# Rewriting the head of an SSM kernel generator: small constants moved to GpSimd, imaginary parts first, the sine table loaded behind the exponential

## The chip, the cores and the metric

The kernel runs on one core of a Trainium2 chip. The time is device time in microseconds of one execution; "before" was run three times. Five engines work side by side, each through its own queue in program order: TensorE (PE, matmuls), VectorE (DVE), ScalarE (ACT), GpSimd (POOL) and SyncE (SP, which here issues nearly all DMAs). They wait for each other by semaphores.

## The reference, cut to what matters

Four layers on x of shape [1, 2048, 512]: A, B, A, B, each added to its input after a layer norm. A is a sliding, dilated local attention (32 heads of 16, window 8, dilation 2). B is a state-space convolution: for each of 512 channels a kernel K of 2048 taps is generated from 128 complex states, and then convolved with the input by an FFT. The change touches only the start of the generation of K, which serves both B layers:

```python
dt = jnp.exp(log_dt)[:, None]
A = A_re + 1j * A_im
logdA = dt * A
dB = dt * (B_re + 1j * B_im)
P = jnp.exp(logdA[:, :, None] * l[None, None, :])     # l = 0 .. 2047
K = jnp.einsum("dn,dnl,dn->dl", Cc, P, dB).real       # Cc = C_re + 1j * C_im
```

## The kernel before

`k_gen` builds K. Its head forms z = exp(dt·A) for all channels and states as one real and one imaginary plane of 128 x 512 (128 states on the partitions, 512 channels in the row). In the order of the code (line numbers of before):

- `build_a_consts` (L83 to L126) makes the constants of layer A ahead of `k_gen`: POOL writes integer ramps with iota, and DVE compares them: `ident` (L88), `nident` (L90), the indicator matrices, `maskrow`, `slot_sel` and `slot_mask` (L95 to L124).
- SP loads `raw_A_re`, `raw_A_im`, `raw_B_re`, `raw_B_im`, `raw_C_re`, `raw_C_im` (L1010), then the first block of x, then fills `w_dram` in DRAM with 4 MB of zeros (L1396, from a zeroed piece of `xnT`, memset at L1380), then the second block of x and the two halves of the query and key weights into `kT_ext` (L245, L246).
- ACT takes the exponential of `log_dt` (`dt_row`, L1025). A matmul with `ident` turns it into a column per channel block (L1027), and DVE multiplies `ident` by it into `dt_diag` (L1029).
- `turned_by` (L1018 to L1022) transposes a raw tile with four matmuls against `dt_diag` or `ident`, so that the A and C parts come out scaled by dt. A_re goes first, then A_im, then B and C.
- ACT forms `a_re` = exp(dt·A_re) (L1040, in the tile `sq_z`) and `turn` = dt·A_im / 2π (L1041, in the tile `ws`). DVE rounds the turn off with a magic number: `t1` from PSUM (L1042), the remainder in `ws` (L1043), its absolute value in `t2` (L1044). ACT takes the two sines (L1045, L1046); the compiler puts the load of the sine table just ahead of the first. DVE multiplies sines and exponential into `sq_z` (L1055, L1056): that is z.
- `build_b_consts` (L610 ff.) makes the index columns for the sine tables of the FFT: POOL iotas, DVE integer steps into `pk` (L621 to L629), DVE steps into `aux` (L633 to L637) and, in its inner function `rest`, into `w_off`, `w_eo` and the two `off_` tiles (L647 to L654), and ACT steps (L641) that use them.

What follows is an order written out by hand, `ORDERK`: one letter per step, and each step issues its instructions on its engine. z is squared eleven times (ACT squares L1059, DVE L1063 and L1066). ACT copies some powers into `pow_t` (L1073, L1078) and others into `B_t` (L1075); SP copies one row of each `pow_t` level beside itself (`power_copy`, L1081). DVE builds two tables of products, `B_t` and `A_t` (all L1084), where each level k of `A_t` reads `pow_t[k]` with its copied row. Between them stand the layer norm of x (statistics and application on ACT, `ln_nb` on DVE L1154), its transposes on PE (L1170), the query and key projections (L1180), and PE's products of the two tables (L1242), which give K. The manual schedule covers DVE, ACT, PE and SP; the placement of POOL's instructions is left to the scheduler.

Of the kernel before, what the change touches and what calls it, by code (L numbers as in the profile page):

```python
# [10 lines left out]
ACT = mybir.ActivationFunctionType  # L11
ALU = mybir.AluOpType
AX = mybir.AxisListType
PSUM = bass.MemoryType.PSUM
F32 = mybir.dt.float32
BF16 = mybir.dt.bfloat16
I32 = mybir.dt.int32
I16 = mybir.dt.int16
ET = mybir.EngineType

P = 128
S = 2048
D = 512
H = 32
DH = 16
W = 8
# [3 lines left out]
EXP_LN = "natural_log_exp_and_others"  # L30
MAN = {ET.DVE, ET.Activation, ET.PE, ET.SP}
SIN_SHRINK = 1.0 - 4e-7
# [50 lines left out]
def build_a_consts(tc, nc, cpool, tpool):  # L83
    c = {}
    it = tpool.tile([P, P], I32, name="iota_id")
    nc.gpsimd.iota(it[:], pattern=[[1, P]], base=0, channel_multiplier=-1)
    ident = cpool.tile([P, P], BF16, name="ident")
    nc.vector.tensor_scalar(ident[:], it[:], 0, None, ALU.is_equal)  # L88
    nident = cpool.tile([P, P], BF16, name="nident")
    nc.vector.tensor_scalar(nident[:], it[:], 0, -1.0, ALU.is_equal, ALU.mult)  # L90
    c["ident"], c["nident"] = ident, nident
    u = tpool.tile([P, 8], I32, name="iota_ind")
    nc.gpsimd.iota(u[:], pattern=[[-16, 8]], base=0, channel_multiplier=1)
    m1 = tpool.tile([P, 8], F32, name="ind_m1")
    nc.vector.tensor_scalar(m1[:], u[:], 0, None, ALU.is_ge)  # L95
    m2 = tpool.tile([P, 8], F32, name="ind_m2")
    nc.vector.tensor_scalar(m2[:], u[:], 15, None, ALU.is_le)
    ind8 = cpool.tile([P, 8], BF16, name="ind8")
    nc.vector.tensor_tensor(ind8[:], m1[:], m2[:], ALU.mult)
    c["ind8"] = ind8  # L100
    rows = cpool.tile([1, P], BF16, name="rows")
    nc.vector.memset(rows[:], 0.0)
    nc.vector.memset(rows[:, 0:1], 1.0)
    c["e0"] = rows[:]
    mv = tpool.tile([1, NA, W], I32, name="iota_mask")
    nc.gpsimd.iota(mv[:], pattern=[[1, NA], [-2, W]], base=0, channel_multiplier=0)
    mrow = cpool.tile([1, NA, W], BF16, name="maskrow")
    nc.vector.tensor_scalar(mrow[:], mv[:], 0, -1e9, ALU.is_lt, ALU.mult)
    c["maskrow"] = mrow
    c["zrow"] = rows[:, 64:128]  # L110
    ind = cpool.tile([P, NDT * H], BF16, name="ind32")
    nc.gpsimd.memset(ind[:], 0.0)
    diag = bass.AP(tensor=ind.tensor, offset=ind[:].offset, ap=[list(ind[:].ap[0]), [H + 8, NDT], [1, 8]])
    nc.vector.tensor_tensor(diag, m1[:].unsqueeze(1).to_broadcast([P, NDT, 8]), m2[:].unsqueeze(1).to_broadcast([P, NDT, 8]), ALU.mult)
    c["ind"] = ind[:].rearrange("p (t h) -> p t h", t=NDT)
    sv = tpool.tile([4, 4, H], I32, name="iota_slot")
    nc.gpsimd.iota(sv[:], pattern=[[-1, 4], [0, H]], base=0, channel_multiplier=1)
    slot = cpool.tile([4, 4, H], BF16, name="slot_sel")
    nc.vector.tensor_scalar(slot[:], sv[:], 0, None, ALU.is_equal)
    c["slot"] = slot[:].rearrange("k a h -> k (a h)")  # L120
    mc = tpool.tile([4, max(NCOL), W], I32, name="iota_slot_mask")
    nc.gpsimd.iota(mc[:], pattern=[[4, max(NCOL)], [-2, W]], base=0, channel_multiplier=1)
    keep = cpool.tile([4, max(NCOL), W], BF16, name="slot_mask")
    nc.vector.tensor_scalar(keep[:], mc[:], 0, -1e9, ALU.is_lt, ALU.mult)  # L124
    c["mask"] = keep
    return c  # L126
# [66 lines left out]
class LayerA:  # L193
# [33 lines left out]
    def front_open(self):  # L227
        tc = self.tc
        self.fctx = ExitStack()
        l = self.layer  # L230
        self.fp = self.fctx.enter_context(tc.tile_pool(name=f"a{l}_front", bufs=2, side="right"))
        self.nc.gpsimd.memset(self.kT[:, :, 0:14, 0:1], 0.0)
# [369 lines left out]
def iota_f32(nc, pool, name, n, step=1, base=0, channel_multiplier=0, parts=P):  # L602
    ti = pool.tile([parts, n], I32, name=name + "_i")
    nc.gpsimd.iota(ti[:], pattern=[[step, n]], base=base, channel_multiplier=channel_multiplier)
    tf = pool.tile([parts, n], F32, name=name)
    nc.scalar.copy(tf[:], ti[:])
    return tf


def build_b_consts(nc, cpool, tmp, w2_dram):  # L610
    C = {}
    EQ = P // 4
    base = tmp.tile([P, EQ, 16], I32, name="w2_base", tag="w2_base")
# [4 lines left out]
    d4i = iota_f32(nc, tmp, "d4i", 2)  # L618
    nc.gpsimd.iota(base[:], pattern=[[16, EQ], [4096, 16]], base=8, channel_multiplier=0)
    t_i = tmp.tile([P, 8], I32, name="pk_t")  # L620
    nc.vector.tensor_scalar(t_i[:, 0:1], pi_i[:], 63, 2, ALU.bitwise_and, ALU.logical_shift_right)  # L621
    nc.vector.tensor_scalar(t_i[:, 1:2], pi_i[:], 6, None, ALU.logical_shift_right)
    nc.vector.tensor_scalar(t_i[:, 2:3], pi_i[:], 3, None, ALU.bitwise_and)
    nc.vector.tensor_scalar(t_i[:, 3:4], pi_i[:], 31, 1, ALU.bitwise_and, ALU.logical_shift_right)
    nc.vector.tensor_scalar(t_i[:, 4:5], pi_i[:], 1, None, ALU.bitwise_and)
    nc.vector.tensor_scalar(t_i[:, 5:6], pi_i[:], 5, 1, ALU.logical_shift_right, ALU.bitwise_and)
    nc.vector.tensor_scalar(t_i[:, 6:7], pi_i[:], 63, 1, ALU.bitwise_and, ALU.logical_shift_left)
    nc.vector.tensor_copy(t_i[:, 7:8], pi_i[:])
    pk = tmp.tile([P, 8], F32, name="pk"); nc.vector.tensor_copy(pk[:], t_i[:])  # L629
# [3 lines left out]
    nc.vector.tensor_tensor(aux[:, 0:1], pk[:, 6:7], rik, ALU.add)  # L633
    nc.vector.tensor_scalar(aux[:, 1:2], pf, 2.0, 1.0, ALU.mult, ALU.add)
    C["p21"] = aux[:, 1:2]
    dmask_m = aux[:, 4:6]
    nc.vector.tensor_scalar(dmask_m, d4i[:], d4m, 2.0 / 4096.0, ALU.is_equal, ALU.mult)  # L637
# [6 lines left out]
    def rest():  # L644
        def off_cols(name, rcol, v00, v10, v01, v11):
            o = tmp.tile([P, 2], F32, name=name)
            nc.vector.tensor_scalar(o[:, 0:1], rcol, float(v10 - v00), float(v00), ALU.mult, ALU.add)  # L647
            nc.vector.tensor_scalar(o[:, 1:2], rcol, float(v11 - v01), float(v01), ALU.mult, ALU.add)
            return o
# [3 lines left out]
        nc.vector.scalar_tensor_tensor(eo[:], ak, 512.0, d4k, ALU.mult, ALU.mult)  # L653
        nc.vector.tensor_tensor(off[:], off[:], eo[:].to_broadcast([P, 2]), ALU.add)  # L654
# [42 lines left out]
    return C, head, rest  # L697
# [282 lines left out]
def k_gen(tc, nc, ident, ins, kd, la, x_v, lnst, zero, b_consts):  # L980
# [3 lines left out]
    with ExitStack() as ctx:  # L984
# [8 lines left out]
        late = {}  # L993
        la.front_open()
# [3 lines left out]
        def nat(ap):  # L998
            return ap.rearrange("p (q g) -> p q g", g=4)
# [8 lines left out]
        for name in ("A_re", "A_im", "B_re", "B_im", "C_re", "C_im"):  # L1008
            raw[name] = sp.tile([P, 4, N], BF16, name="raw_" + name)
            nc.sync.dma_start(raw[name][:], ins[name].rearrange("(t p) n -> p t n", p=P))  # L1010
# [4 lines left out]
        nc.gpsimd.memset(Bt[:, 0, :, 0, :], 1.0)  # L1015
        nc.gpsimd.memset(Bt[:, 1, :, 0, :], 0.0)

        def turned_by(name, rhs):  # L1018
            pt = pst.tile([P, 4, P], F32, name="pt")
            for t in range(4):  # L1020
                nc.tensor.matmul(pt[:, t, :], lhsT=raw[name][:, t, :], rhs=rhs(t), start=True, stop=True)
            return pt[:].rearrange("p g q -> p q g")  # L1022

        dtr = sp.tile([4, P], BF16, name="dt_row")
        nc.scalar.activation(dtr[:], ldt[:], ACT.Exp)  # L1025
        pdt = pst.tile([P, 4, P], F32, name="pt")
# [4 lines left out]
        C, head, rest = b_consts(sp)  # L1031
# [5 lines left out]
        a_re, turn = cur[0][:, 0], ws[:, 2]  # L1037
        p_re = turned_by("A_re", by_dt)
        p_im = turned_by("A_im", by_dt)
        nc.scalar.activation(nat(a_re), p_re, ACT.Exp)  # L1040
        nc.scalar.mul(nat(turn), p_im, 1.0 / TWO_PI)  # L1041
        nc.vector.tensor_scalar(nat(t1[:]), p_im, 1.0 / TWO_PI, MAGIC, ALU.mult, ALU.add)  # L1042
        nc.vector.scalar_tensor_tensor(turn, t1[:], MAGIC, turn, ALU.subtract, ALU.subtract)  # L1043
        nc.vector.scalar_tensor_tensor(t2[:], turn, -1.0, turn, ALU.mult, ALU.max)  # L1044
        nc.scalar.activation(sn, turn, ACT.Sin, scale=TURN)  # L1045
# [3 lines left out]
        steps, w2_store = rest()  # L1049
# [303 lines left out]
def kernel(  # L1353
# [27 lines left out]
    with tc.tile_pool(name="ctmp", bufs=1) as tmp:  # L1381
        consts = build_a_consts(tc, nc, cpool, tmp)
# [3 lines left out]
    nc.gpsimd.memset(lnst["mh"][:], -0.5)  # L1386
# [6 lines left out]

    with tc.manual_schedule(engines=MAN):
        C = k_gen(tc, nc, consts["ident"], ins, kd, la, x_v, lnst,
                  lambda: nc.sync.dma_start(w2_dram.rearrange("p e c -> p (e c)").rearrange("p (n x) -> p n x", x=1024),  # L1396
                                            zt.unsqueeze(1).to_broadcast([P, P * P // 1024, 1024])),
                  lambda sp: build_b_consts(nc, cpool, sp, w2_dram))
# [61 lines left out]
    with tc.manual_schedule(engines=MAN):  # L1460
        la.front_open()
        ln, agg, pts = {}, {}, {}
# [88 lines left out]
```

## Time and profile before

| what | value |
|---|---|
| median of 3 runs (lowest, highest) | 412.89 us (412.36, 413.35) |
| the profiled execution: time, span | 412.14 us, 410.3 us |
| busy: DVE, ACT, PE | 384.2 us (94%), 326.7 us (80%), 322.0 us (78%) |
| busy: POOL | 46.0 us (11%), 52 instructions |
| granted TensorE clock, mean | 0.938 |
| DMA | 54.17 MB, mean 132 GB/s |

A line of the timeline reads: start in us, duration in us, engine and line, operation, output tile <- input tiles, shape and type of each, number of instructions, and in brackets the idle time of that engine just before, with what ended it. A line of the windows holds, for a stretch A:B, its length, then the busy time and number of instructions of PE, PE weight loads, DVE, ACT and POOL, then the granted TensorE clock, the mean busy share of the 16 DMA engines and GB/s. A line of the DMA issues ends with the median time from issue to landing.

### The profile page before, as it was taken

What the parts mean: (1) busy time and instruction counts of PE and PEld (TensorE: products, weight loads), DVE (VectorE), ACT (ScalarE), POOL (GpSimd) and SP (SyncE); (2) the same over time, 40 slices, a digit from 0 to 9 for tenths busy, and PEclk for the clock granted to TensorE, in tenths of its full rate; (3) what the DMA queues carried; (4) which work ended last, traced back from release to release, by engine and by line L of the source; (5) the groups of instructions that cost most, each with busy time, mean ns of one, the idle gap of its engine ahead of it and who ended that gap; (6) DMA issues with size and microseconds to landing.
All of it is one profiled execution on the core that took longest, in us unless ns stands there. A gap on an engine that the chain in (4) does not pass through costs nothing.

```text
span 410.3 us, 14708 instructions
## 1 busy us (share of the span) xinstructions
PE 322.0 (78%) x6467; PEld 227.0 (55%) x6513; DVE 384.2 (94%) x498; ACT 326.7 (80%) x562; POOL 46.0 (11%) x52
## 2 busy tenths in 40 slices
PE   2000168899899888789988889999998999897794
PEld 2000026567535555566887778543466677566784
DVE  7999999999999999998899989888988999989993
ACT  5999999897556589898999978874656658889972
POOL 3000400000299300001400000000000020000000
PEclk9555569999999999999999999999999999999998
DMA  7930742113015856583245595830043028504516
GB/s 229 388 113 13 84 82 72 33 41 91 13 39 123 213 169 180 159 339 105 71 164 182 180 307 141 311 127 2 0 116 92 3 71 343 158 3 150 161 30 181
DMA packets 62322, 54.17 MB, mean 132 GB/s; under 512 B 33869, under 2 KB 50738, under 8 KB 60978
## 3 DMA queue, kind: packets, MB, share of 16 engines
q1 hardware_dynamic: 62250, 53.22, 42.8%
q8 instruction: 51, 0.84, 0.9%
q14 instruction: 13, 0.11, 0.1%
q10 hardware_dynamic: 8, 0.00, 0.0%
HBM read 30.15 MB, written 13.24 MB: 106 GB/s over the span
## 4 chain that ended last, share of the span: by engine, by line
PE 35%; ACT 18%; DVE 17%; issue 7%; DMA 3%; SPq 2%; DVEq 0%; ACTq 0%
PE pk L1242 5%; DVE pav L458 5%; PE pq L389 5%; DVE prod L333 4%; ACT a1s L774 4%; PE pp L1180 4%; ACT ub L851 3%; PE pp L273 3%; PE pq L216 3%; PE pq L494 2%; DVE t L835 2%; PE pb L869 2%; PE po L483 2%; PE L L341 2%; DMA v_ext<-v_ext 1%
## 5 line engine op out<-in xcount | busy, mean ns | idle before, releaser
L458 DVE TENSOR_TENSOR pav<-attn,v_ext 128x4096 bf16<-128x4096 bf16 (+1 forms) x34 | 73.1, 2168 | 1.2 <-DMA v_ext<-v_ext 0.8
L333 DVE TENSOR_TENSOR prod<-qT,kT_ext 128x4096 bf16<-128x4096 bf16 x29 | 67.1, 2337 | 1.6 <-ACT qT L218 1.1
L1170 PE MATMUL pt<-ident,x_blk 128*128 128x128 bf16 x64 | 6.3, 241 | 42.6 <-DMA w_dram<-w_q 41.1
L1084 DVE TENSOR_TENSOR A_t<-A_t,pow_t 128x1024 bf16<-128x1024 bf16 (+4 forms) x46 | 38.2, 870 | 0.2
L483 PEld LDWEIGHTS <-pav 64*128 64x128 bf16 x1664 | 26.2, 95 | 15.1 <-DVE pav L458 8.5
L483 PE MATMUL po<-ident,pav 64*128 64x64 bf16 x1664 | 29.0, 190 | 6.6 <-DVE pav L458 3.9
L494 PE MATMUL pq<-wop,oT 128*128 128x512 bf16 x122 | 31.6, 379 | 2.5 <-issue 1.9
L851 ACT CAST ub<-pb 128x1024 bf16<-128x1024 f32 x32 | 32.3, 1091 | 0.1
L391 ACT CAST v_ext<-pq 128x512 bf16<-128x512 f32 x32 | 18.8, 586 | 17.0 <-PE pq L389 16.0
L792 PE MATMUL pb<-a1s,w_sb 128*128 128x64 bf16 x768 | 28.0, 193 | 5.4 <-ACT a1s L774 2.3
L389 PE MATMUL pq<-wv,xnT 128*128 128x512 bf16 x121 | 30.1, 379 | 0.6 <-ACT kgs L1250 0.3
L1180 PE MATMUL pp<-xnT,kT_ext 128*128 128x512 bf16 x87 | 25.0, 405 | 7.0 <-ACT qT L1185 2.9
L1170 PEld LDWEIGHTS <-x_blk 128*128 128x128 bf16 x64 | 4.8, 108 | 45.0 <-ACT x_blk L188 43.6
L792 PEld LDWEIGHTS <-w_sb 128*128 128x128 bf16 x768 | 25.0, 98 | 8.0 <-issue 5.2
L774 DVE CAST a1s<-pb 128x1024 bf16<-128x1024 f32 x21 | 25.0, 1217 | 4.1 <-PE pb L785 4.1
L774 ACT CAST a1s<-pb 128x1024 bf16<-128x1024 f32 x27 | 26.4, 1052 | 2.3 <-PE pb L785 2.2
L1242 PEld LDWEIGHTS <-A_t 128*64 128x64 bf16 (+1 forms) x512 | 21.8, 103 | 4.1 <-issue 0.6
L1242 PE MATMUL pk<-B_t,A_t 128*64 128x84 bf16 (+1 forms) x512 | 23.6, 201 | 0.1
L216 PE MATMUL pq<-xnT,kT_ext 128*128 128x512 bf16 x89 | 22.8, 379 | 0.5 <-issue 0.3
L494 PEld LDWEIGHTS <-oT 128*128 128x128 bf16 x128 | 12.4, 98 | 14.0 <-ACT oT L485 1.1
L485 ACT CAST oT<-po 128x512 bf16<-128x512 f32 x26 | 15.0, 577 | 6.0 <-PE po L483 5.9
L389 PEld LDWEIGHTS <-xnT 128*128 128x128 bf16 x128 | 11.6, 97 | 14.1 <-issue 1.9
(258 smaller groups left out, 871.9 us busy)
## 6 DMA issues: line engine op xcount, KB each, us to landing
w_sb<-w_dram SPq DMA_DIRECT2D x8, 1024.0 KB, 6.7
w_dram<-xnT SPq DMA_DIRECT2D x1, 4096.0 KB
kf_ring<-kf_dram SPq DMA_DIRECT2D x13, 256.0 KB, 4.4
kf_ring<-kf_dram SPq DMA_DIRECT2D x26, 128.0 KB, 3.7
v_ext<-v_ext SPq DMA_DIRECT2D x4, 784.0 KB, 6.3
x_blk<-in_A_x_dram SPq DMA_DIRECT2D x4, 512.0 KB, 3.9
kT_ext<-in_A_wqkv_dram SPq DMA_DIRECT2D x4, 512.0 KB, 9.9
x_sb<-in_A_x_dram SPq DMA_DIRECT2D x4, 512.0 KB, 5.2
```

The lines of the kernel that those rows point to most:

```text
L216: nc.tensor.matmul(pq[:], lhsT=self.wqk[:, dt, ft * P:(ft + 1) * P], rhs=self.xnT[:, dt, q * 512:(q + 1) * 512], start=(dt == 0), stop=(dt ...
L333: nc.vector.tensor_tensor(pr, self.qT[q][:, ft].unsqueeze(1).to_broadcast([P, W, 4, P]), kap, ALU.mult)
L389: nc.tensor.matmul(pp[:], lhsT=xnT[:, dt, a * P:(a + 1) * P], rhs=wv[:, dt, :], start=(dt == 0), stop=(dt == NDT - 1))
L458: nc.vector.tensor_tensor(pv[:, i], attn[:, n % 4].unsqueeze(2).to_broadcast([P, W, DH // parts, H]), vap, ALU.mult)
L483: nc.tensor.matmul(po[:, h, 0, i * nt + ft, :], lhsT=pvf[rows, i, w, ft * P:(ft + 1) * P], rhs=ident[rows, rows], start=(w == 0 and ft + i ...
L494: nc.tensor.matmul(pw[:], lhsT=oT[:, ftp, :], rhs=self.wo[:, ftp, :], start=False, stop=(ftp == NDT - 1))
L774: (self.nc.scalar.copy if eng == "act" else self.nc.vector.tensor_copy)(dst, src)
L792: nc.tensor.matmul(p2[:, j, :], lhsT=self.w2[:, ec * EC + j, :], rhs=a1s[:, ec * EC + j, :], start=True, stop=True)
L851: nc.scalar.copy(ub[:], p2)
L1084: return lambda: nc.vector.tensor_tensor(*args)
L1180: nc.tensor.matmul(pps[kind, b, ft][:], lhsT=la.wqk[:, dt, c:c + P], rhs=la.xnT[:, dt, b * 512:(b + 1) * 512], start=(dt == 0), stop=(dt = ...
L1242: nc.tensor.matmul(o, lhsT=lhs, rhs=Bt[:, ri, c * CH + ql].rearrange("p b g -> p (b g)"), start=(not half and j % 4 == 0 and ri == 0), sto ...
```

## The change

- `build_a_consts` moves into `k_gen` and is split in three. At once come the iota for `ident` and, now on POOL, `ident` itself; `iotas()` issues the other ramps behind the exponential of `log_dt`; `rest()` (called `a_rest`) makes the remaining constants, now on POOL, behind those of `build_b_consts`.
- `build_b_consts` is split likewise: its iotas first, then `keys` (DVE, into `pk`), `keyed` (`aux`, now on POOL) and `rest` (offsets, now on POOL; one fused DVE step becomes two POOL steps).
- POOL joins the engines of the manual schedule for `k_gen`, so that its instructions stand in the order of the code. The memsets of `kT_ext` (`front_zero`), `ln_mh` and `B_t` come behind the iotas.
- A_im is loaded and transposed ahead of A_re; `turn` stands ahead of the exponential on ACT.
- `t1` reads `turn` from SBUF instead of A_im from PSUM.
- The load of the sine table is written out, behind the exponential.

On the engines' queues: 20 instructions fewer on DVE, 21 more on POOL, as many as before on PE, ACT and SP. The scheduler puts the memset of the tile `Wp` between the first iota and `ident`, and that of `WpJ` among the offsets. `ORDERK` is unchanged.

```diff
-def build_a_consts(tc, nc, cpool, tpool):
-    c = {}
+def build_a_consts(nc, cpool, tpool, c):
     it = tpool.tile([P, P], I32, name="iota_id")
     nc.gpsimd.iota(it[:], pattern=[[1, P]], base=0, channel_multiplier=-1)
     ident = cpool.tile([P, P], BF16, name="ident")
-    nc.vector.tensor_scalar(ident[:], it[:], 0, None, ALU.is_equal)
+    nc.gpsimd.tensor_scalar(ident[:], it[:], 0, None, ALU.is_equal)
...
+    def iotas():
+        nc.gpsimd.iota(u[:], pattern=[[-16, 8]], base=0, channel_multiplier=1)
...
+    def rest():
+        nc.gpsimd.tensor_scalar(nident[:], it[:], 0, -1.0, ALU.is_equal, ALU.mult)
+        m1 = tpool.tile([P, 8], F32, name="ind_m1")
+        nc.gpsimd.tensor_scalar(m1[:], u[:], 0, None, ALU.is_ge)
...
+    return iotas, rest
...
 def build_b_consts(nc, cpool, tmp, w2_dram):
...
+    def keys():
+        nc.vector.tensor_scalar(t_i[:, 0:1], pi_i[:], 63, 2, ALU.bitwise_and, ALU.logical_shift_right)
...
+    def keyed():
+        nc.gpsimd.tensor_tensor(aux[:, 0:1], pk[:, 6:7], rik, ALU.add)
...
-            nc.vector.tensor_scalar(o[:, 0:1], rcol, float(v10 - v00), float(v00), ALU.mult, ALU.add)
+            nc.gpsimd.tensor_scalar(o[:, 0:1], rcol, float(v10 - v00), float(v00), ALU.mult, ALU.add)
...
-        nc.vector.scalar_tensor_tensor(eo[:], ak, 512.0, d4k, ALU.mult, ALU.mult)
-        nc.vector.tensor_tensor(off[:], off[:], eo[:].to_broadcast([P, 2]), ALU.add)
+        nc.gpsimd.tensor_scalar(eo[:], ak, 512.0, None, ALU.mult)
+        nc.gpsimd.tensor_tensor(eo[:], eo[:], d4k, ALU.mult)
+        nc.gpsimd.tensor_tensor(off[:], off[:], eo[:].to_broadcast([P, 2]), ALU.add)
...
+        iotas, a_rest = a_consts(sp)
+        ident = la.c["ident"]
...
-        for name in ("A_re", "A_im", "B_re", "B_im", "C_re", "C_im"):
+        for name in ("A_im", "A_re", "B_re", "B_im", "C_re", "C_im"):
...
         nc.scalar.activation(dtr[:], ldt[:], ACT.Exp)
+        iotas()
+        C, keys, keyed, head, rest = b_consts(sp)
+        la.front_zero()
+        nc.gpsimd.memset(lnst["mh"][:], -0.5)
+        nc.gpsimd.memset(Bt[:, 0, :, 0, :], 1.0)
+        nc.gpsimd.memset(Bt[:, 1, :, 0, :], 0.0)
...
+        keys()
+        keyed()
+        steps, w2_store = rest()
+        a_rest()
...
+        p_im = turned_by("A_im", by_dt)
         p_re = turned_by("A_re", by_dt)
-        p_im = turned_by("A_im", by_dt)
-        nc.scalar.activation(nat(a_re), p_re, ACT.Exp)
         nc.scalar.mul(nat(turn), p_im, 1.0 / TWO_PI)
-        nc.vector.tensor_scalar(nat(t1[:]), p_im, 1.0 / TWO_PI, MAGIC, ALU.mult, ALU.add)
+        nc.vector.tensor_scalar(t1[:], turn, MAGIC, None, ALU.add)
         nc.vector.scalar_tensor_tensor(turn, t1[:], MAGIC, turn, ALU.subtract, ALU.subtract)
         nc.vector.scalar_tensor_tensor(t2[:], turn, -1.0, turn, ALU.mult, ALU.max)
+        nc.scalar.activation(nat(a_re), p_re, ACT.Exp)
+        nc.scalar.preload_act_table_set(SIN)
         nc.scalar.activation(sn, turn, ACT.Sin, scale=TURN)
...
-    with tc.manual_schedule(engines=MAN):
-        C = k_gen(tc, nc, consts["ident"], ins, kd, la, x_v, lnst,
+    with tc.manual_schedule(engines=MAN_ALL):
+        C = k_gen(tc, nc, lambda sp: build_a_consts(nc, cpool, sp, consts), ins, kd, la, x_v, lnst,
```

More of the change, by code (lines that the diff above doesn't have):

```diff
@@ L30 @@
 EXP_LN = "natural_log_exp_and_others"
+SIN = "trig_and_small"
 MAN = {ET.DVE, ET.Activation, ET.PE, ET.SP}
+MAN_ALL = MAN | {ET.Pool}
 SIN_SHRINK = 1.0 - 4e-7
@@ L87, in build_a_consts @@
     ident = cpool.tile([P, P], BF16, name="ident")
-    nc.vector.tensor_scalar(ident[:], it[:], 0, None, ALU.is_equal)
+    nc.gpsimd.tensor_scalar(ident[:], it[:], 0, None, ALU.is_equal)
     nident = cpool.tile([P, P], BF16, name="nident")
-    nc.vector.tensor_scalar(nident[:], it[:], 0, -1.0, ALU.is_equal, ALU.mult)
     c["ident"], c["nident"] = ident, nident
[L92 to L100, printed above, removed]
     rows = cpool.tile([1, P], BF16, name="rows")
@@ L104, in build_a_consts @@
     c["e0"] = rows[:]
+    c["zrow"] = rows[:, 64:128]
+    u = tpool.tile([P, 8], I32, name="iota_ind")
     mv = tpool.tile([1, NA, W], I32, name="iota_mask")
[L106 to L110, printed above, removed]
-    ind = cpool.tile([P, NDT * H], BF16, name="ind32")
-    nc.gpsimd.memset(ind[:], 0.0)
@@ L113, in build_a_consts @@
[L113 to L126, printed above, removed]
+    sv = tpool.tile([4, 4, H], I32, name="iota_slot")
@@ new lines, in build_a_consts @@
+    mc = tpool.tile([4, max(NCOL), W], I32, name="iota_slot_mask")
+    ind = cpool.tile([P, NDT * H], BF16, name="ind32")
+    def iotas():
+        nc.gpsimd.iota(u[:], pattern=[[-16, 8]], base=0, channel_multiplier=1)
+        nc.gpsimd.iota(mv[:], pattern=[[1, NA], [-2, W]], base=0, channel_multiplier=0)
+        nc.gpsimd.iota(sv[:], pattern=[[-1, 4], [0, H]], base=0, channel_multiplier=1)
+        nc.gpsimd.iota(mc[:], pattern=[[4, max(NCOL)], [-2, W]], base=0, channel_multiplier=1)
+        nc.gpsimd.memset(ind[:], 0.0)
@@ new lines, in rest @@
+    def rest():
+        nc.gpsimd.tensor_scalar(nident[:], it[:], 0, -1.0, ALU.is_equal, ALU.mult)
+        m1 = tpool.tile([P, 8], F32, name="ind_m1")
+        nc.gpsimd.tensor_scalar(m1[:], u[:], 0, None, ALU.is_ge)
+        m2 = tpool.tile([P, 8], F32, name="ind_m2")
+        nc.gpsimd.tensor_scalar(m2[:], u[:], 15, None, ALU.is_le)
+        mrow = cpool.tile([1, NA, W], BF16, name="maskrow")
+        nc.gpsimd.tensor_scalar(mrow[:], mv[:], 0, -1e9, ALU.is_lt, ALU.mult)
+        ind8 = cpool.tile([P, 8], BF16, name="ind8")
+        nc.gpsimd.tensor_tensor(ind8[:], m1[:], m2[:], ALU.mult)
+        diag = bass.AP(tensor=ind.tensor, offset=ind[:].offset, ap=[list(ind[:].ap[0]), [H + 8, NDT], [1, 8]])
+        nc.gpsimd.tensor_tensor(diag, m1[:].unsqueeze(1).to_broadcast([P, NDT, 8]), m2[:].unsqueeze(1).to_broadcast([P, NDT, 8]), ALU.mult)
+        slot = cpool.tile([4, 4, H], BF16, name="slot_sel")
+        nc.gpsimd.tensor_scalar(slot[:], sv[:], 0, None, ALU.is_equal)
+        keep = cpool.tile([4, max(NCOL), W], BF16, name="slot_mask")
+        nc.gpsimd.tensor_scalar(keep[:], mc[:], 0, -1e9, ALU.is_lt, ALU.mult)
+        c["ind8"], c["maskrow"], c["mask"] = ind8, mrow, keep
+        c["ind"] = ind[:].rearrange("p (t h) -> p t h", t=NDT)
+        c["slot"] = slot[:].rearrange("k a h -> k (a h)")
@@ L231, in front_open, with front_zero @@
         self.fp = self.fctx.enter_context(tc.tile_pool(name=f"a{l}_front", bufs=2, side="right"))
+    def front_zero(self):
         self.nc.gpsimd.memset(self.kT[:, :, 0:14, 0:1], 0.0)
@@ L612, in build_b_consts @@
     EQ = P // 4
-    base = tmp.tile([P, EQ, 16], I32, name="w2_base", tag="w2_base")
     pi_i = tmp.tile([P, 1], I32, name="p_i")
@@ L618, in build_b_consts @@
     d4i = iota_f32(nc, tmp, "d4i", 2)
+    base = tmp.tile([P, EQ, 16], I32, name="w2_base", tag="w2_base")
     nc.gpsimd.iota(base[:], pattern=[[16, EQ], [4096, 16]], base=8, channel_multiplier=0)
     t_i = tmp.tile([P, 8], I32, name="pk_t")
[L621 to L629, printed above, removed]
+    pk = tmp.tile([P, 8], F32, name="pk")
     ak, rik, d4k, cm, rim, d4m = (pk[:, j:j + 1] for j in range(6))
@@ L632, in build_b_consts @@
     aux = cpool.tile([P, 8], F32, name="aux")
-    nc.vector.tensor_tensor(aux[:, 0:1], pk[:, 6:7], rik, ALU.add)
-    nc.vector.tensor_scalar(aux[:, 1:2], pf, 2.0, 1.0, ALU.mult, ALU.add)
     C["p21"] = aux[:, 1:2]
     dmask_m = aux[:, 4:6]
-    nc.vector.tensor_scalar(dmask_m, d4i[:], d4m, 2.0 / 4096.0, ALU.is_equal, ALU.mult)
+    def keys():
+        nc.vector.tensor_scalar(t_i[:, 0:1], pi_i[:], 63, 2, ALU.bitwise_and, ALU.logical_shift_right)
+        nc.vector.tensor_scalar(t_i[:, 1:2], pi_i[:], 6, None, ALU.logical_shift_right)
+        nc.vector.tensor_scalar(t_i[:, 2:3], pi_i[:], 3, None, ALU.bitwise_and)
+        nc.vector.tensor_scalar(t_i[:, 3:4], pi_i[:], 31, 1, ALU.bitwise_and, ALU.logical_shift_right)
+        nc.vector.tensor_scalar(t_i[:, 4:5], pi_i[:], 1, None, ALU.bitwise_and)
+        nc.vector.tensor_scalar(t_i[:, 5:6], pi_i[:], 5, 1, ALU.logical_shift_right, ALU.bitwise_and)
+        nc.vector.tensor_scalar(t_i[:, 6:7], pi_i[:], 63, 1, ALU.bitwise_and, ALU.logical_shift_left)
+        nc.vector.tensor_copy(t_i[:, 7:8], pi_i[:])
+        nc.vector.tensor_copy(pk[:], t_i[:])
+    def keyed():
+        nc.gpsimd.tensor_tensor(aux[:, 0:1], pk[:, 6:7], rik, ALU.add)
+        nc.gpsimd.tensor_scalar(aux[:, 1:2], pf, 2.0, 1.0, ALU.mult, ALU.add)
+        nc.gpsimd.tensor_scalar(dmask_m, d4i[:], d4m, 2.0 / 4096.0, ALU.is_equal, ALU.mult)
     f1t = [tmp.tile([P, P], I32, name=f"f1_t{j}") for j in range(2)]
@@ L646, in off_cols @@
             o = tmp.tile([P, 2], F32, name=name)
-            nc.vector.tensor_scalar(o[:, 0:1], rcol, float(v10 - v00), float(v00), ALU.mult, ALU.add)
-            nc.vector.tensor_scalar(o[:, 1:2], rcol, float(v11 - v01), float(v01), ALU.mult, ALU.add)
+            nc.gpsimd.tensor_scalar(o[:, 0:1], rcol, float(v10 - v00), float(v00), ALU.mult, ALU.add)
+            nc.gpsimd.tensor_scalar(o[:, 1:2], rcol, float(v11 - v01), float(v01), ALU.mult, ALU.add)
             return o
@@ L695, in rest @@
         return steps, w2_store
-    return C, head, rest
+    return C, keys, keyed, head, rest
 def low16(ap):
@@ L977, with k_gen @@
 NROW = 641
-def k_gen(tc, nc, ident, ins, kd, la, x_v, lnst, zero, b_consts):
+def k_gen(tc, nc, a_consts, ins, kd, la, x_v, lnst, zero, b_consts):
     B_L = (0, 1, 2, 3, 4, 5, 6, 7, 256, 258, 260, 262, 512, 516, 768, 772, 1024, 1280, 1536, 1792, 2048)
@@ L1014, in k_gen @@
         la.front_w()
-        nc.gpsimd.memset(Bt[:, 0, :, 0, :], 1.0)
-        nc.gpsimd.memset(Bt[:, 1, :, 0, :], 0.0)
         def turned_by(name, rhs):
@@ L1030, in k_gen @@
         by_dt, plain = (lambda t: dtd[:, t, :]), (lambda t: ident[:])
-        C, head, rest = b_consts(sp)
+        keys()
+        keyed()
+        steps, w2_store = rest()
+        a_rest()
         ws = sp.tile([P, 3, 4 * P], F32, name="ws")
@@ L1048, in k_gen @@
             f()
-        steps, w2_store = rest()
         T = {name: turned_by(name, by_dt if name[0] == "C" else plain) for name in ("B_re", "B_im", "C_re", "C_im")}
@@ L1380 @@
     nc.vector.memset(zt, 0.0)
-    with tc.tile_pool(name="ctmp", bufs=1) as tmp:
-        consts = build_a_consts(tc, nc, cpool, tmp)
+    consts = {}
     lnst = dict(s1=cpool.tile([P, NA], F32, name="ln_s1"), s2=cpool.tile([P, NA], F32, name="ln_s2"),
@@ L1385 @@
                 mh=cpool.tile([P, 4], F32, name="ln_mh"))
-    nc.gpsimd.memset(lnst["mh"][:], -0.5)
     kd = dram.tile([NROW, D], BF16, name="kd_dram")
@@ L1461 @@
         la.front_open()
+        la.front_zero()
         ln, agg, pts = {}, {}, {}
```

## The prediction

> **What bounds the kernel now.** I read the page first, then the timeline of the first 27 us on every engine, the windows of DMA activity there, the DMA issues with their landing times, and the chain that ended last. The page:
>
> ```profile
> span 410.3 us, 14708 instructions
> ...
> DVE  7999999999999999998899989888988999989993
> ```
>
> VectorE (DVE) is busy from the second of the 40 slices on; only the first, where the change lies, has slack. A saved microsecond there counts if DVE's later work really starts earlier, so the head has to be read instruction by instruction (start, duration, then engine and line; a bracket names the idle time before it and who ended it):
>
> ```profile
> 1.50 1.64 DVE L88 TENSOR_SCALAR ident<-iota_id 128x128 bf16<-128x128 int32 x1
> ...
> 2.40 0.65 POOL L619 IOTA w_base<- 128x512 int32 x1
> 2.63 0.31 ACT L1025 ACTIVATE dt_row<-ldt 4x128 bf16<-4x128 bf16 x1
> ...
> 3.82 0.67 DVE L1029 TENSOR_TENSOR dt_diag<-ident,pt 128x512 bf16<-128x512 bf16 x1
> ...
> 5.65 0.59 ACT L1041 ACTIVATE ws<-pt 128x512 f32<-128x512 f32 x1
> ...
> 7.00 0.69 DVE L1043 SCALAR_TENSOR_TENSOR ws<-t,ws 128x512 f32<-128x512 f32 x1
> ...
> 7.78 1.28 ACT L1045 ACT_TABLE_LOAD   x1 [1.53 <-DVE ws L1043]
> ...
> 9.07 0.63 ACT L1045 ACTIVATE ws<-ws 128x512 f32<-128x512 f32 x1
> ...
> 9.74 0.69 DVE L1055 TENSOR_TENSOR sq_z<-sq_z,ws 128x512 f32<-128x512 f32 x1 [0.69 <-ACT ws L1045]
> ```
>
> The chain is dt_row, a small matmul, dt_diag, eight matmuls, exponential and turn on ScalarE (ACT), three DVE steps, the sine table load, two sines, sq_z. The identity took 1.64 us, by all appearance because it could not run beside GpSimd's (POOL's) string of iotas: it ended at 3.14, just after w_base at 3.05, and nident, queued behind it, 0.06 us later. Then seven small constant steps hold dt_diag to 3.82. The table load waits for ws although it needs nothing from it.
>
> Next, where DVE first meets a DMA that the head does not drive. L1084 at 26.35 multiplies by row 0 of pow_t, which an SP copy (L1081) writes; two of those copies, issued at 20.82 and at 28.36, with their landing times:
>
> ```profile
> 25.48 0.95 DVE L1084 TENSOR_TENSOR B_t<-B_t 128x1536 bf16<-128x1536 bf16 x1
> 26.35 0.29 DVE L1084 TENSOR_TENSOR A_t<-A_t,pow_t 128x256 bf16<-128x256 bf16 x1
> ```
>
> ```profile
> pow_t<-pow_t SPq DMA_DIRECT2D x1, 128.0 KB, 5.1
> ```
>
> ```profile
> pow_t<-pow_t SPq DMA_DIRECT2D x1, 128.0 KB, 2.2
> ```
>
> So the first copy landed at 20.82 + 5.1 = 25.9, only 0.4 us before DVE used it, and it took 2.9 us longer than the third. The windows say why (last columns: DMA share and GB/s):
>
> ```profile
> 22.00:23.00 1.00, 0.00 (x0) 0.00 (x0) 0.97 (x3) 1.00 (x3) 0.00 (x0) 0.50 1.04 284
> 23.00:24.00 1.00, 0.00 (x0) 0.00 (x0) 1.00 (x3) 1.00 (x2) 0.00 (x0) 0.50 0.16 45
> 24.00:25.00 1.00, 0.00 (x0) 0.00 (x0) 1.00 (x3) 1.00 (x4) 0.00 (x0) 0.50 0.60 134
> 25.00:26.00 1.00, 0.00 (x0) 0.00 (x0) 1.00 (x2) 1.00 (x4) 0.00 (x0) 0.50 0.08 18
> 26.00:28.00 2.00, 0.00 (x0) 0.00 (x0) 2.00 (x5) 2.00 (x4) 0.00 (x0) 0.50 0.00 0
> ```
>
> From 2 to 23 us all 16 DMA engines drain raw loads, x_blk, the 4 MB zero fill of w_dram and two weight loads; a tail on about one engine (0.08 of 16) lasts to 26.0, and the copy's piece on it comes behind that backlog. From 26.4 to 60.1 the timeline shows not one idle bracket on DVE, and the chain that ended last begins there:
>
> ```profile
> 60.14 0.08 DVE ln_nb L1154
> ```
>
> **The change, part by part.** *Identity to POOL, constants off DVE.* POOL runs iota_id (to 1.07), the Wp memset (0.23 to 0.34), then ident. POOL's price for 128 columns is not in the trace. Nearest rows: a 128x128 iota 0.27; 128x512 tensor_scalars at 0.77 (L190) and 1.18 (the k_perm pair of L714 that took 2.35), four times as long. I take 0.4; ident is ready between 1.6 and 2.6. It is needed when the dt_row weights are in, 2.99 + 0.10 = 3.09, since dt_row waits for the first table load, which covers it; past 3.09 it costs one for one. The matmul (0.16) ends at 3.25, dt_diag starts near 3.3 instead of 3.82: **0.5 us earlier** (0.4 to 0.57).
>
> *Iotas behind ident.* ACT's casts of e, aidx and d4i stand ahead of turn. d4i_i ended at 2.44; with ident and Wp ahead and two memsets moved behind, it ends at 3.1 (4.1 with the dear ident), its cast by 3.4 to 4.5; turn starts at 4.6. Hidden.
>
> *Imaginary parts first, table behind exp.* From the end of dt_diag (4.49) to the table load (7.78) were 3.29 us. Now: first matmul group and hand-over 0.67 (4.49 to 5.16), turn, exp 0.49 later (5.16 to 5.65), its 0.60, hand-over 0.02: the load starts at 1.78. **1.5 us earlier.** The sine needs ws: turn ends at 1.26, t1 takes 0.69 as before from PSUM or as little as 0.41 (128x512 bf16 from SBUF, L190 on DVE), I take 0.5; ws 0.72: done near 2.5, while the load ends at 3.06. That 0.5 us is the cover for delays on DVE. A load straight behind an activation is in the trace at 43.92, 0.02 after s_WpJ, and costs 1.28. "ScalarE: Activation LUTs" of the Trainium skill (What ACT_TABLE_LOAD costs) adds a drain of about 1.38 to each switch; by it this term would be an estimated 0.1 instead of 1.5 and the head's gain 0.6; the trace at 43.92 disagrees.
>
> *SP.* The A_im and A_re loads swap. The second one landed at 1.23 + 2.9 = 4.13; A_re's weights are now wanted near 4.4. The order behind them is unchanged.
>
> *Work given to POOL.* Three aux steps and eight offsets leave DVE; they lay in its waits (5.21 to 5.57, and 8.34 to 9.05 while the sine was pending), so this is worth nothing on DVE. w_off is due at ACT's L641, 13.55 before and some 11.5 after; it is POOL's eighth step behind pk (5.1). At 0.12 (the smallest iotas) to 0.78 each (64x64 tensor_tensor, L682) plus a memset of 0.23 it is ready between 6.3 and 11.6; by size I take 0.2, 6.9. The other constants and the B_t, kT_ext and ln_mh memsets are needed later.
>
> *Sum at the head:* 0.5 + 1.5 = 2.0; L1055 starts at 7.7.
>
> *What is late next.* Everything on DVE moves by 2.0 up to L1084 at 26.35, which could start at 24.3. Its copy is issued at 18.8 instead of 20.82, still behind the same backlog, whose bytes and start do not depend on the head. So I put its landing at 25.9 again: DVE waits 1.6 us, starts at 25.97, and **0.4 us** of the 2.0 is left. ACT, in step with DVE through the squares, waits there as well, and DVE without idle time cannot make it up before 60.14. The landing is the open price: earliest 18.8 + 2.2 = 21.0, which hinders nothing (gain 2.0); at the late end, the three timed runs differ by 0.99, so I allow 0.5 either way: gain 0 to 0.9.
>
> The profiled execution took 412.14 (span 410.3 and 1.84 around it), 0.75 under the median; it would become 411.7, and the median 412.89 becomes **412.5**. A measurement of this kernel can tell about 0.2%, 0.83 us, from no change, so this lies within it.
>
> **Rivals.** *The whole gain arrives.* The tail on one DMA engine is seen in one execution; without it the backlog ends at 23.0 and the copy has landed before 24.3. Then 412.89 - 2.0 = 410.9, or up to 412.0 where the tail is shorter. For: the other engines were done by 23 to 23.5. Against: with the DMA engines full for 21 us, uneven shares are to be expected again.
>
> *POOL's string of small steps starves t1, ws and t2: slower.* In the changed kernel POOL is busy from pk on (5.1) with 20 small steps and a memset, just when t1 arrives at 5.2. For: ident on DVE stood still through nine consecutive POOL instructions. Against: at 43 to 48 us DVE's tensor_tensors ran on time (0.94, 0.68) beside L682, and POOL was the one stretched (1.78 against 0.78). At 0.2 each the string ends at 5.1 + 4.2 = 9.3; t1, ws and the sine follow, 1.1 later, at 10.4 instead of 9.07: 1.4 slower, 414.3. It turns at 8.0 (0.13 a step); beyond that it is loss one for one, as the DMA no longer hides it. The rule "Who interferes with whom" in "SBUF — State Buffer" of the Trainium skill speaks against the change here: a VectorE step in a two-port mode, or with two SBUF inputs against a reading GpSimd step, and a GpSimd step exclude each other, and the loser blocks for a whole instruction. By that rule each of t1, ws, t2 loses one POOL step at a time, an estimated 0.2 each, inside the cover of 0.5; ident's 1.5 us shows that it can be more.
>
> *The head does not get faster.* If ident or the iotas on POOL are dearer than 1.5 us, dt_diag stays at 3.8 or turn moves back; then 412.9.
>
> **How the numbers follow.** The copy's landing holds the gain to 0 to 0.9: 0.43, time 412.5. The gain arrives whole or more than 0.83 of it: 0.35, 410.9 to 412.0. Starved: 0.16, 413.8 to 415.5. No gain at the head: 0.06, 412.9. Faster by over 0.2%: 0.35; within: 0.43 + 0.06 = 0.49; slower: 0.16. The range takes the first, second and last case with their spread, 410.8 to 413.3, and leaves out the starved one; the likeliest case alone has 412.0 to 412.9.
>
> **What would show it.** Right: dt_diag near 3.3, the table load near 5.7, L1055 (now L1077) near 7.7, then an idle bracket of about 1.6 us on DVE before the first A_t multiplication by pow_t, at 25.9, named for the DMA. Wrong: no bracket there and ln_nb at 58.1 (the gain is whole); t1 or ws lasting over a microsecond beside POOL (starved); ident on POOL ending after 3.1.

## The result, and the profile after

The changed kernel took 409.90 us in the median of 4 runs (409.61 to 410.55), the kernel before 412.88 (412.36 to 413.35): ratio 0.993, 95% interval 0.9907 to 0.9952. Two larger comparisons of the same two kernels, made with the experiments below, gave 0.9952 (0.9936 to 0.9969) and 0.9946 (0.9928 to 0.9964), which are 2.0 and 2.2 us. The profiled executions took 412.14 and 409.99: 2.15 less. So the change makes the kernel faster by about 2 us (the intervals of the two larger comparisons run from 1.3 to 3.0); the prediction said 0.4 and a range whose lower end was 410.8. The kernel before was timed in four sets of runs, with medians of 412.88, 411.75, 412.66 and 411.67: its level moves by about 1 us from set to set, so only differences and ratios within a set count.

The page after, the two lines that answer to those shown of before:

```profile
span 408.2 us, 14705 instructions
...
DVE  6999999999999999998899989888989999989983
```

The timeline of the head after the change (start, duration, engine, line; a bracket names idle time and who ended it):

```profile
1.21 0.55 POOL L90 TENSOR_SCALAR ident<-iota_id 128x128 bf16<-128x128 int32 x1
2.64 0.31 ACT L1038 ACTIVATE dt_row<-ldt 4x128 bf16<-4x128 bf16 x1
3.22 0.69 DVE L1048 TENSOR_TENSOR dt_diag<-ident,pt 128x512 bf16<-128x512 bf16 x1 [1.65 <-PE pt L1046]
4.59 0.60 ACT L1062 ACTIVATE ws<-pt 128x512 f32<-128x512 f32 x1 [1.25 <-PE pt L1034]
5.08 0.59 ACT L1066 ACTIVATE sq_z<-pt 128x512 f32<-128x512 f32 x1
5.22 0.44 DVE L1063 TENSOR_SCALAR t<-ws 128x512 f32<-128x512 f32 x1 [0.43 <-ACT ws L1062]
5.69 1.28 ACT L1067 ACT_TABLE_LOAD   x1
5.69 0.69 DVE L1064 SCALAR_TENSOR_TENSOR ws<-t,ws 128x512 f32<-128x512 f32 x1
6.98 0.63 ACT L1068 ACTIVATE ws<-ws 128x512 f32<-128x512 f32 x1
7.65 0.69 DVE L1077 TENSOR_TENSOR sq_z<-sq_z,ws 128x512 f32<-128x512 f32 x1 [0.53 <-ACT ws L1068]
```

`dt_diag` starts at 3.22 instead of 3.82, the table load at 5.69 instead of 7.78, `sq_z` at 7.65 instead of 9.74: the head is 2.09 shorter. The table load has lost its bracket of 1.53: it begins behind the exponential, while DVE still forms `ws`.

The place where the prediction put the new wait, in the same view, and the first copy of `pow_t` among the DMA issues (x2: the stretch shown holds two copies; a shorter one with the first alone gives 5.7 as well):

```profile
23.41 0.95 DVE L1106 TENSOR_TENSOR B_t<-B_t 128x1536 bf16<-128x1536 bf16 x1
24.50 0.29 DVE L1106 TENSOR_TENSOR A_t<-A_t,pow_t 128x256 bf16<-128x256 bf16 x1
```

```profile
pow_t<-pow_t SPq DMA_DIRECT2D x2, 128.0 KB, 5.7
```

The copy, issued at 18.74, landed at 18.74 + 5.7 = 24.44, not at 25.9. Before, the multiplication started 0.87 after the start of the step ahead of it (25.48 to 26.35, with no wait); from 23.41 that gives 24.28, so it now starts 0.2 late. The windows of DMA activity show the tail behind which the prediction put the copy (last columns: DMA share and GB/s):

```profile
23.00:24.00 1.00, 0.00 (x0) 0.00 (x0) 1.00 (x2) 1.00 (x4) 0.00 (x0) 1.00 0.65 151
24.00:25.00 1.00, 0.00 (x0) 0.00 (x0) 0.87 (x3) 1.00 (x3) 0.00 (x0) 1.00 0.07 16
25.00:26.00 1.00, 0.00 (x0) 0.00 (x0) 1.00 (x3) 1.00 (x2) 0.00 (x0) 1.00 0.00 0
```

It is over by 25.0, where in the profile of before it lasted to 26.0. From there the gain is kept: 1.85 at this multiplication, and at the first link of the chain that ended last, which stood at 60.14,

```profile
58.30 0.08 DVE ln_nb L1176
```

it is 1.84; the span is 2.1 shorter. (In the timeline, which the numbers on `ln_nb` below are taken from, this step starts at 58.22, and at 60.06 before.)

### The profile page after: what moved, and what is told of

Its sections match the earlier page's. It is cut to its first block, busy times and chain, and to the rows that moved or that the text cites. A ratio compares the mean times of both kernels' runs of the same rounds, so it can differ in the third digit from the quotient of the medians.

```text
span 408.2 us, 14705 instructions
## 1 busy us (share of the span) xinstructions
PE 322.2 (79%) x6467; PEld 226.9 (56%) x6513; DVE 381.0 (93%) x478; ACT 327.0 (80%) x562; POOL 55.7 (14%) x73
## 4 chain that ended last, share of the span: by engine, by line
PE 36%; ACT 15%; DVE 13%; DMA 10%; issue 6%; SPq 4%; DVEq 0%; ACTq 0%
PE pq L396 5%; PE pk L1264 5%; DVE pav L465 4%; PE pp L1202 4%; DMA v_ext<-v_ext 3%; PE pq L221 3%; ACT a1s L787 3%; PE pp L280 3%; ACT ub L864 3%; DMA w_sb<-w_dram 2%; PE L L348 2%; PE pq L501 2%; DMA kf_ring<-kf_dram 2%; PE pb L882 2%; DVE prod L340 2%
## 5 line engine op out<-in xcount | busy, mean ns | idle before, releaser
L176 POOL TENSOR_TENSOR ln_rstd<-ln_rstd,ln_mh 128x4 f32<-128x4 f32 x2 | 3.9, 1971 | 125.5 <-DVE ln_rstd L175 125.5
```

## The experiments

Theory 1: the gain is the head's 2.0, made of an earlier table load (1.5) and an earlier `dt_diag` (0.5), and it passes whole when the first copy of `pow_t` lands by 24.3; the landing moves from execution to execution. Theory 2: the landing caps the gain near 0.4, and the rest of the measured 3 us came from elsewhere.

**The kernel before, again.** No edit.

> The unchanged kernel of before, profiled a second time. Theory A (the head's gain passes on one for one; the copy of pow_t row 0 lands at a time that varies by over a microsecond between executions): the copy's landing differs from 25.9 by 0.5 to 2 us; where it lands after 26.3, DVE shows an idle bracket before L1084 and the execution is longer by as much. Rival B (the landing is fixed by the backlog): 25.9 within 0.2 again and no bracket. Time 412.2 to 413.4 by both.

Measured: 411.55 (12 runs) against 411.75 (35 runs of the same kernel), ratio 0.9998 (0.9981 to 1.0014). The copy in this profile, from its DMA issues:

```profile
pow_t<-pow_t SPq DMA_DIRECT2D x1, 128.0 KB, 3.7
```

Issued at 20.82 as before, it landed at 24.5, 1.4 earlier than in the execution on which the prediction was built. DVE still began the multiplication where it had:

```profile
26.36 0.28 DVE L1084 TENSOR_TENSOR A_t<-A_t,pow_t 128x256 bf16<-128x256 bf16 x1
```

Its own work set that: in this kernel the landing moved by 1.4 and nothing showed it. The median of the first three runs, 412.89, was 1.1 above that of these 35, which spread from 410.68 to 414.33. The absolute times in the expectations are counted from 412.89 and have to be read as differences.

**The changed kernel, again.** No edit.

> The changed kernel, profiled a second time. Theory A: the copy lands anywhere from 23.5 to 26, DVE waits for it 0 to 1.6 us, time 409.6 to 410.6. Rival B (something in the change itself made the copy land at 24.4): landing 24.4 within 0.2, wait 0.1, time within 0.3 of 409.9.

Measured: 409.58 (12 runs) against 411.75, ratio 0.9952 (0.9936 to 0.9969). In its profile the predicted wait is there; the timeline and the DMA issue:

```profile
25.53 0.29 DVE L1106 TENSOR_TENSOR A_t<-A_t,pow_t 128x256 bf16<-128x256 bf16 x1 [1.19 <-DMA pow_t<-pow_t]
```

```profile
pow_t<-pow_t SPq DMA_DIRECT2D x1, 128.0 KB, 6.7
```

Landing at 25.4, 1.19 of idle time named for the copy, and `ln_nb` at 59.25, 1.03 later than in the first profile after the change (58.22). Of the head's 2.09 only 0.81 is left at `ln_nb`, against 60.06 before. The cap exists, then, in some executions. This one nevertheless had a span of 408.0 against 408.2: from `ln_nb` to the end it took 348.8, the first one 350.0. Over all thirteen profiles this later part lies between 348.8 and 351.1, and both ends are profiles of the changed kernel, so no single time can show what the wait costs.

**The order alone.** The kernel before with the A_im load and transposes first, `turn` ahead of the exponential, `t1` from SBUF and the written-out table load (not shown: the swapped names of the loads and the definition of `SIN`):

```diff
+        p_im = turned_by("A_im", by_dt)
         p_re = turned_by("A_re", by_dt)
-        p_im = turned_by("A_im", by_dt)
-        nc.scalar.activation(nat(a_re), p_re, ACT.Exp)
         nc.scalar.mul(nat(turn), p_im, 1.0 / TWO_PI)
-        nc.vector.tensor_scalar(nat(t1[:]), p_im, 1.0 / TWO_PI, MAGIC, ALU.mult, ALU.add)
+        nc.vector.tensor_scalar(t1[:], turn, MAGIC, None, ALU.add)
...
+        nc.scalar.activation(nat(a_re), p_re, ACT.Exp)
+        nc.scalar.preload_act_table_set(SIN)
```

> Before, with only the order changed: A_im loaded and transposed first, turn ahead of the exponential, t1 from SBUF, table load behind the exponential; the constants stay on DVE. Sum of the prediction: 1.5 us at the head, sq_z (first product) near 8.2, time 411.4 against 412.9. If the constants are what counts: under 0.5. If the copy of pow_t binds at 25.9: 412.5.

Measured: 410.29 (12 runs), ratio 0.9962 (0.9944 to 0.998), 1.6 us. In its timeline, no bracket stands before this line:

```profile
8.21 0.69 DVE L1057 TENSOR_TENSOR sq_z<-sq_z,ws 128x512 f32<-128x512 f32 x1
```

1.53 of the head's 2.09 come from the order. The copy landed at 24.6 in this execution; DVE, 0.56 behind the changed kernel, did not wait.

**The constants alone.** The changed kernel with these lines put back to the old order, so that only the identity, the constants and the iotas stand as in the change.

> The changed kernel with the old order (A_re first, exponential ahead of turn, t1 from PSUM, no load behind the exponential): only the constants and the identity are moved to GpSimd. Sum of the prediction: 0.5 us at the head, dt_diag near 3.3, sq_z near 9.2, time 412.4. If moving the constants is worth more than its place on the path (less load on DVE later): 411.5 or less. If GpSimd's steps delay t1 to t2: 413 or more.

Measured: 410.70 (12 runs), ratio 0.9985 (0.9969 to 1.0001), 0.6 us, with the interval just reaching no change.

```profile
9.18 0.69 DVE L1076 TENSOR_TENSOR sq_z<-sq_z,ws 128x512 f32<-128x512 f32 x1 [1.30 <-ACT ws L1067]
```

0.56 at `sq_z`; with 1.53 the sum is 2.09, what both together gave: at the head the two parts are independent. In time, 1.6 + 0.6 = 2.2 agrees with the whole gain, though each of these times has an interval of about 0.7 either way.

**One more megabyte ahead of the copy**, in the changed kernel and in the kernel before: 1 MB of zeros to an unused DRAM tile, on SP behind the weight loads (not shown: the tile, `pad_dram`, and the definition of `zero`, which fills it when its argument is 1).

```diff
         la.front_w()
+        zero(1)
```

> The changed kernel with one megabyte more of zeros (into a DRAM tile that nobody reads) queued on SP between the weight loads and the first copy of pow_t; at 400 GB/s that is 2.6 us of all DMA engines. Theory A (the copy lands when the backlog ahead of it has drained, and DVE stands at the first A_t multiplication until then): landing 27 to 28.5, an idle bracket of 2.7 to 4.2 us on DVE named for the copy, sines and sq_z as early as in the changed kernel (7.65), and a time 2 to 3 us above the changed kernel, so within 1 us of before. Rival (a wait there is made up later, or does not end the kernel): time within 0.7 us of the changed kernel.

> Before with the same megabyte. Theory A: the copy lands at 27 to 28.5 as in the changed kernel with the megabyte, DVE (there at 26.36) waits 0.7 to 2.1 us, time 0.7 to 2.1 above before, and the change is then worth less than 0.7 us. Rival (the change's 2 us do not depend on the copy): 2 us slower than the changed kernel with the megabyte.

Measured, changed kernel: 413.65 (12 runs) against 412.66 for the kernel before without the megabyte (24 runs), ratio 1.0017 (0.9997 to 1.0036). Before with the megabyte: 413.26, ratio 1.0019 (0.9996 to 1.0041). The two timelines at the multiplication, the changed kernel first:

```profile
28.07 0.29 DVE L1107 TENSOR_TENSOR A_t<-A_t,pow_t 128x256 bf16<-128x256 bf16 x1 [3.73 <-DMA pow_t<-pow_t]
```

```profile
27.13 0.29 DVE L1085 TENSOR_TENSOR A_t<-A_t,pow_t 128x256 bf16<-128x256 bf16 x1 [0.70 <-DMA pow_t<-pow_t]
```

The head of the changed kernel still ended 2.09 early (`sq_z` at 7.64), and all of it was lost at the copy: the change then shows no gain (413.65 against 413.26), where without the megabyte it is worth about 2 us. The kernel before lost 0.8 in time, with an interval of -0.2 to 1.7, beside a wait of 0.70. (The two copies, issued at 18.73 and 20.82, took 9.2 and 6.2 and landed at 27.9 and 27.0 behind the same bytes: again a difference of 0.9.) So the prediction's mechanism is right: a landing some 3 us later turns the gain into none.

**One weight load behind the copy.** In the changed kernel, the query half of the weights, the second of the two weight loads, is queued behind the first copy.

```diff
-        la.front_w()
+        nc.sync.dma_start(la.wqk[:, :, D:2 * D], la.wsrc[:, :, D:2 * D])
...
+            if k == 0:
+                nc.sync.dma_start(la.wqk[:, :, 0:D], la.wsrc[:, :, 0:D])
```

> The changed kernel with the second weight load (512 KB, query half of wqk, needed by the projections near 56 us) queued behind the first copy of pow_t instead of ahead of it: 1.3 us less ahead of the copy. Theory A: landing 23 to 24.5, no idle bracket on DVE before the first A_t multiplication (at 24.3), sq_z unchanged at 7.65; the mean of the waits seen so far (0.1 and 1.2), some 0.6 us, is gained: 0.5 to 0.7% below before. Rival (the waits are made up later): the same time as the changed kernel.

Measured: 409.97 (7 runs) against 412.66, ratio 0.9932 (0.9905 to 0.9959). The multiplication starts 0.87 after the step before it (23.39), so without a wait:

```profile
24.26 0.28 DVE L1108 TENSOR_TENSOR A_t<-A_t,pow_t 128x256 bf16<-128x256 bf16 x1
```

`ln_nb` came to 57.98. This profile gives no landing time for the copy, so the expected 23 to 24.5 is not tested. Nor does one profile without a wait show that the cap is gone: the identity experiment below, with the weight load in its old place, has none either (24.26). The ratio's interval overlaps those of the changed kernel, and the comparisons are of different sets, so what the wait costs on average is not resolved: the gain is 2.8 us here and 2.0 to 2.2 with the load in its old place.

**The first table load early as well.** On top of the last edit, the load of the exponential's table is written ahead of ACT's own DMA for `log_dt`.

```diff
+        nc.scalar.preload_act_table_set("exp_and_others")
```

> As e7, and the first table load stands ahead of the load of log_dt on ACT instead of behind it. Theory A (the table load at 1.34 to 2.62 gates dt_row, so the head still has slack): the load starts near 0.75 and ends near 2.05, dt_row starts when log_dt lands, sq_z earlier by up to 0.55 us, and the time falls by as much, since the copy of pow_t no longer binds. Rival (log_dt's own landing gates dt_row, and its issue is now later): dt_row no earlier than 2.6, or later, no gain or a loss of up to 0.6.

Measured: 409.14 (6 runs), ratio 0.9911 (0.988 to 0.9941), 3.7 us below the kernel before; the difference from the last kernel is within the intervals, but the timeline shows a part of it:

```profile
0.73 1.28 ACT L1021 ACT_TABLE_LOAD   x1 [0.73 <-PEq L1559]
2.12 0.31 ACT L1039 ACTIVATE dt_row<-ldt 4x128 bf16<-4x128 bf16 x1
```

`dt_row` starts 0.52 earlier than with the change alone, `sq_z` 0.42 earlier (7.23), `ln_nb` at 57.56. The median of this version is the lowest of all; that it beats the kernel before is clear, that it beats the changed kernel (0.9936 to 0.9969 and 0.9928 to 0.9964) is not, since the intervals overlap.

**The identity back on DVE**, all else as changed; one execution.

> The changed kernel with the identity alone back on DVE. Theory A (DVE's step on the ramp cannot run beside GpSimd's unbroken string of iotas and memsets, whoever needs it): ident starts near 1.5 and ends only where w_base or a memset behind it ends, 3.0 to 3.4 or later, although DVE has nothing else to do; dt_diag at 3.4 or later, sq_z at 7.8 or later. Rival (the 1.64 us of before were ident's own price, or DVE's queue): a few tenths, ending by 1.9, or 1.64 again from 1.5 to 3.14 whatever GpSimd does.

Measured: 409.17. The timeline:

```profile
1.31 0.60 DVE L90 TENSOR_SCALAR ident<-iota_id 128x128 bf16<-128x128 int32 x1
```

It ended at 1.91, while POOL's string of iotas and memsets ran without a gap from 0.84 to beyond 3.6. It had time to spare: `dt_diag` again started at 3.22. The explanation that `ident` on DVE cannot run until the string ends falls; five or six of POOL's instructions ran beside it, and no run shows what it takes with none. With everything else moved, `ident` itself could have stayed on DVE: the 0.6 comes from taking `nident` and seven constant steps out from between `ident` and `dt_diag`, and from `ident` not lasting 1.64.

**Without the written-out table load**, all else as changed; one execution.

> The changed kernel without the written-out table load; the compiler puts it ahead of the first sine again. Theory A (of the 1.5 us of the order, the load behind the exponential is the larger part): the load waits for ws, which is done at 6.38, so it starts near 6.45 instead of 5.69, the sine near 7.75, sq_z near 8.4 instead of 7.65: 0.75 us lost at the head, 0.75 kept. Rival (the load need not be written out, since imaginary parts first are enough): load near 5.7, sq_z at 7.65.

Measured: 410.46.

```profile
6.46 1.28 ACT L1067 ACT_TABLE_LOAD   x1 [0.80 <-DVE ws L1064]
```

The load waits for `ws` again and `sq_z` moves from 7.65 to 8.42. Of the order's 1.53, 0.77 therefore hang on that one line. The rest is left to the order of loads and transposes, `turn` ahead of the exponential and the cheaper `t1`, which no run separates.

**The changed kernel, a third time.** No edit.

> The changed kernel timed and profiled once more, to size the gain: the first comparison said 3.0 us (interval 2.0 to 3.8), the second 2.0 (1.3 to 2.6). Theory A (head's 2.1 less a wait for the copy of 0 to 1.2): ratio between 0.9945 and 0.9965, landing 24.3 to 26. Rival (something beyond the head is worth another microsecond): ratio 0.993 or lower.

Measured: 409.17 (8 runs) against 411.67 (13 runs), ratio 0.9946 (0.9928 to 0.9964). The profiled execution was a long one, 411.17, and its head was that of the others: `sq_z` at 7.64, copy landed at 24.35, `ln_nb` at 58.16. What made this execution long lies behind the head: from `ln_nb` to the end it took 351.1, against 350.0 and 348.8 in the two other profiles of this kernel.

## Why the prediction was wrong

**The head's sum was right.** 0.5 + 1.5 = 2.0 was forecast, 0.60 + 1.49 = 2.09 measured, and the two parts alone gave 0.56 and 1.53. (0.60 is just above the 0.4 to 0.57 that the first term allowed.) `t1` was put at 0.5 and took 0.44; `ident` on POOL at 0.4 and took 0.55, ending at 1.76, well before it was needed. The iotas and the casts stayed hidden.

**The table load.** It began 0.02 after the exponential ended and the sine 0.01 after the load: 1.28 and no more. "ScalarE: Activation LUTs" of the Trainium skill (What ACT_TABLE_LOAD costs) adds about 1.38 of drain to each switch; none shows here, and the head's gain of 2.09 instead of the estimated 0.6 goes against it.

**The step that failed: "So I put its landing at 25.9 again".** That the copy waits behind the backlog, that it is what DVE meets next, and that `ln_nb` follows it one for one were all right; the second profile after the change and the two kernels with a megabyte more show it. The term was mis-sized: 25.92 was the landing in one execution, and the latest of all those seen without extra bytes. The nine profiles of kernels with this backlog (times in us):

| kernel | copy issued | landed | multiplication starts |
|---|---|---|---|
| before | 20.82 | 25.9 | 26.35 |
| before, again | 20.82 | 24.5 | 26.36 |
| changed | 18.74 | 24.4 | 24.50 |
| changed, again | 18.73 | 25.4 | 25.53 |
| changed, third | 18.73 | 24.3 | 24.43 |
| order alone | 19.30 | 24.6 | 24.83 |
| constants alone | 20.26 | 24.4 | 25.79 |
| identity on DVE | 18.72 | 24.1 | 24.26 |
| no written-out load | 19.51 | 24.5 | 25.05 |

Seven of the nine land between 24.1 and 24.6. DVE is ready at 24.26 to 24.28 in the changed kernel and in the one with the identity on DVE, so it started 0 to 0.2 late in three of these four profiles and 1.3 late in one, where the prediction had 1.6.

**The allowance was taken from the wrong spread.** I let the landing vary by half the difference of the timed runs, 0.5 either way. But in the kernel before DVE does not come to the copy until 26.35: any landing earlier than that leaves the time untouched, so those times held no information on it. The rival *the whole gain arrives*, with 0.35, described what mostly happened, and its difference of 2.0 is right. Its reason was a shorter tail, and that is what the profiles show. That the first comparison gave 3.0, a microsecond more than the head can give, no profile explains.

**Starvation did not happen; the stretching went the other way.** The timeline after shows POOL's one-column steps beside `ws` (5.69 to 6.38) and `t2` (6.42 to 7.12):

```profile
5.72 0.71 POOL L659 TENSOR_SCALAR w_off<-pk 128x1 f32<-128x1 f32 x1
6.39 0.19 POOL L660 TENSOR_SCALAR w_off<-pk 128x1 f32<-128x1 f32 x1
6.54 0.68 POOL L665 TENSOR_SCALAR w_eo<-pk 128x1 f32<-128x1 f32 x1
```

A step of 0.19 takes about 0.7 when a DVE step of 128 x 512 is running, and DVE's steps keep their 0.69. That agrees with "SBUF — State Buffer" of the Trainium skill (Who interferes with whom), by which the loser blocks for a whole instruction; here POOL lost. POOL's string ended at 14.4 instead of the 9.3 of the prediction's rival, and it held nobody up: `w_off` was complete at 7.80, forecast for 6.9, and its user on ACT started at 11.46. One small DVE step did grow: the cast into `pk` took 0.36 instead of 0.17, beside POOL's memset of `B_t`.

**What stays open.** Why `ident` took 1.63 to 1.64 in all four profiles in which `nident` follows it on DVE, and 0.60 without `nident`, beside a POOL string of the same kind, in the identity experiment: DVE's own queue and the different string are both possible, and no run separates them. What makes the tail on the DMA engine end anywhere from 24.2 to 26.0. And whether the first comparison's 3.0 holds anything beyond the 2.0 to 2.2 of the later two, whose intervals it overlaps.

## What to carry to other kernels

When a transfer lands shortly before it is used and nobody waits for it, its landing in one profile is a sample, not a constant, and the kernel's times say nothing about its spread; compute the capped and the uncapped gain and get a second profile of the same kernel before choosing. The sine table's load ran while DVE still formed the sine's input, so write such a load out behind the last user of the old table (0.77 us here). Bulk transfers that are needed late are worth queueing behind a small copy that is needed soon: a megabyte ahead of it cost a wait of 3.73 here, while the gain from moving half a megabyte behind it is not resolved.

## What the runs showed of the hardware

- After some 20 us with all DMA engines busy, a tail of about one engine's work (a share of 0.07 to 0.08 of 16 at its end) lasted 1 to 3 us longer, and its end moved by about 1 us between executions of one kernel. The small copy queued behind landed with it: at 25.9 with a tail to 26.0, at 24.4 with one to 24.5, at 25.4 with one to some 25.5. Whether the tail is what was left of the bulk transfers or the copy's own piece on a late engine, the windows do not tell.
- The granted clock was 0.50 at 50 to 56 us in the profile before and 1.00 after, but single matmuls lasted the same: the 128 x 128 transposes of x 308 and 310 ns on average, the 128 x 512 products behind them 626 and 625 ns. Where the mean over the span was 0.93 or 0.94, an early stretch of records at 0.50, in which PE has little to do, made most of the difference. From `ln_nb` to the end these three executions took 350.2, 349.3 and 351.1; the other ten, at 0.99 to 1.00, took 348.8 to 350.5, so these few profiles do not tie the length to the mean clock.
- A table load on ACT ran from 0.73 to 2.01 beside ACT's own DMA issue (0.76 to 1.31): the two do not exclude each other.
